# LSH attention and two MoE layers on one core: the exponential between the two casts in every third attention step

## The chip, the cores and the metric

The kernel runs on one core of a Trainium2 chip. The metric is device time in microseconds (us). Engine names in the rows: PE is TensorE's matrix multiplication, PEld its loads of the stationary operand, DVE VectorE, ACT ScalarE, POOL GpSimd, SP the engine that issues most transfers. TensorE multiplies and transposes into PSUM; VectorE and ScalarE read PSUM and do the rest of the arithmetic.

## The reference

Attention with a bucket mask comes first, then two feed-forward layers on its output. Shapes: 2 batches, 8 heads, 768 positions, head size 64; 1536 tokens, model width 512, hidden width 2048; everything in 32-bit floats.

```python
mask = q_bucket[:, :, :, None] == k_bucket[:, :, None, :]
scores = scale * np.matmul(q, k.transpose(0, 1, 3, 2))
scores = np.where(mask, scores, -1000000000.0)
scores = scores - np.max(scores, axis=-1, keepdims=True)
attn = np.exp(scores)
attn = attn / (np.sum(attn, axis=-1, keepdims=True) + 1e-09)
return np.matmul(attn, v).astype(np.float32)
...
h = x @ w_in
g = h * (1.0 / (1.0 + np.exp(-1.702 * h)))
return (g @ w_out).astype(np.float32)
```

The second layer is like the first with another activation. The buckets are the signs of six projections of each query and key.

## The kernel before

The attention runs as one loop over 96 score steps: 16 heads with 6 tiles of 128 queries each, and four more steps to drain. Score step `i` makes one tile of 128 queries by 768 keys. What belongs to one tile is spread over five steps, so that every step holds work of several tiles:

- `qk(i + 1)` (L613): four matrix products into one of two PSUM tiles `s`, scores and mask together.
- `clamp(i)` (L625, VectorE): reads `s`, writes the tile `p` in SBUF and the row minimum `mn`.
- `expo(i)` (L638, ScalarE): the exponential of `p` in place, with the row sums. It needs the clamp.
- `trp(g, t)` (L676 and L683): three transposes on TensorE, 128 columns of each of the three tiles `p` of the group `g`, into a PSUM tile `pt`, of which there are three buffers; then a cast on ScalarE to the high part `pth`. The three tiles of group `g` are those of score steps 3g, 3g+1 and 3g+2, so the first transposes of a group need the exponential of the last step of the three. Each step transposes two such 128-column pieces, called A and B here.
- `trl(g, t)` (L688, VectorE): the low part `ptl` = `pt` minus `pth`. It needs the cast.
- `pv(g, t)` (L700, L701): in the step after, the products of both parts with the values, into the PSUM tile `u`. When the sixth piece of a group is done, `u_out` copies `u` out on ScalarE (L712). This falls into steps with number 0 modulo 3, behind their exponential.

Every engine takes its instructions in the order of the program, and the schedule is written out by hand: a string of letters gives the order within a step. A and B are the two `trp`, a and b the two `trl`, C the clamp, E the exponential, T the list of other work that is due at this step, Q the next scores, P and R the two `pv`.

The list of other work holds, for each head from number 2 on, the products with the bucket projections and the mask comparison of the head (L493 on TensorE, `mk` L513 on VectorE). They fall into every sixth step, always one with number 2 modulo 3, and take a `pt` buffer too. Once per pair of heads it holds the transposition of the row sums (L657) and their reciprocal (L653). From step 47 on it prepares the first two weight tiles: their operations on VectorE (L238, L243) fall into steps 47, 59, 71 and 83, which are 2 modulo 3 as well. Behind the loop come the two feed-forward layers, whose weights, activations and sums are ordered by a list of due times.

Of the kernel before, what the change touches and what calls it, by code (L numbers as in the profile page):

```python
# [41 lines left out]
def lsh_attention_moe_kernel(  # L42
# [291 lines left out]
    def r_in(m, f, k0=0, k1=KD):  # L334
        if k0 == 0:
            pool, tag = mps["h"], f"h{f % 2}"
            if (m, f // 2) == (0, 1):
                pool, tag = (mps["q"], "Y") if f % 2 else (mps["h"], "y0")
            h_t[m, f] = pool.tile([P, CH], F32, tag=tag, name="h")
        h = h_t[m, f]  # L340
        wh, wl = w_t[m, f, 0]
        n = 3 * k0
        for kk in range(k0, k1):
            wk = slice(kk * P, (kk + 1) * P)
            for a, x in ((wh, xr_hi), (wh, xr_lo), (wl, xr_hi)):
                nc.tensor.matmul(  # L346
                    h, a[:, wk], x[:, kk], start=(n == 0), stop=(n == 3 * KD - 1)
                )
                n += 1

    def attention():
        with ExitStack() as es:
# [67 lines left out]
            def keep_warm(n, cols):  # L420
                t = ps_t.tile([P, 512], F32, tag="pt", name="warm")
                for _ in range(n):
                    nc.tensor.matmul(t[:, :cols], ones[:, :P], ones[:, :cols], start=True, stop=True)
# [179 lines left out]
            def qk(i, parts=(0, 1), fs=(0, 1)):  # L603
                n, t = divmod(i, NT)
                kh, qx, qb, kb, _ = opnd[n]
                if 0 in parts and 0 in fs:
                    st_t[i] = ps_s.tile([P, 2, 512], F32, tag="s", name="s")
                s = st_t[i]
                c = slice(t * P, (t + 1) * P)
                both = (qx, kh, True), (qb, kb, False)  # L610
                for a, bb, st in [both[x] for x in parts]:
                    for f in fs:
                        nc.tensor.matmul(  # L613
                            s[:, f, :HS],
                            a[:, c],
                            bb[:, f * HS : (f + 1) * HS],
                            start=st,
                            stop=not st,
                        )

            def clamp(i):
                s = st_t[i]
                sb = pp.tile([P, 2, HS], F32, tag="p", name="p")
                mn = sm.tile([P, 1], F32, tag="mn", name="mn")
                nc.vector.tensor_scalar(  # L625
                    sb, s[:, :, :HS], NEG, None, ALU.min, ALU.min, accum_out=mn
                )
                st_t[i] = (sb, mn)

            def expo(i):  # L630
                sb, mn = st_t.pop(i)
                n, t = divmod(i, NT)
                p = sb.rearrange("p a b -> p (a b)")
                u, h = divmod(n, 2)
                if t == 0 and h == 0:
                    z_t[u] = sm.tile([P, 2 * NT], F32, tag="z", name="z", bufs=2)
                zc = NT * h + t
                nc.scalar.activation(  # L638
                    p,
                    p,  # L640
                    AF.Exp,
                    bias=mn,
                    scale=-1.0,
                    accum_out=z_t[u][:, zc : zc + 1],
                )
                p_t[i] = p
# [26 lines left out]
            def trp(g, t):  # L673
                ptile = ps_t.tile([P, 512], F32, tag="pt", name="pt")
                for j in range(3):
                    nc.tensor.transpose(  # L676
                        ptile[:, j * P : (j + 1) * P],
                        p_t[3 * g + j][:, t * P : (t + 1) * P],
                        ident,
                    )  # L680
                hi = ptp.tile([P, HS], F32R, tag="pth", name="pth")
                lo = ptp.tile([P, HS], F32R, tag="ptl", name="ptl")
                nc.scalar.copy(hi, ptile[:, :HS])  # L683
                pt_t[g, t] = (hi, lo, ptile)

            def trl(g, t):
                hi, lo, ptile = pt_t[g, t]
                nc.vector.tensor_sub(lo, ptile[:, :HS], rnd(hi))  # L688
                if t == NT - 1:
                    for j in range(3):  # L690
                        p_t.pop(3 * g + j)

            def pv(g, t):
                n, f = divmod(g, 2)
                hi, lo, _ = pt_t.pop((g, t))
                if t == 0:
                    u_t[g] = ps_u.tile([P, 512], F32, tag="u", name="u")
                ut = u_t[g]
                vv = opnd[n][4][0]
                nc.tensor.matmul(ut[:, :HS], vv[:, t, :], hi, start=(t == 0), stop=False)  # L700
                nc.tensor.matmul(ut[:, :HS], vv[:, t, :], lo, start=False, stop=(t == NT - 1))  # L701
                if t == NT - 1:
                    u_out(g)
# [47 lines left out]
            second[2]()  # L751
            LAG = 3
            ORDER = "ACaBbETQPR"
            NZ = 5
            NZL = 2
            PVLAG = LAG + 1
# [2 lines left out]
            def at(step, f, *args):  # L759
                todo.setdefault(step, []).append((f, args))  # L760
# [30 lines left out]
            for u in range(NHD // 2):  # L791
                zs = 2 * NT * (u + 1)
                nz = NZ if u < NHD // 2 - 1 else NZL
                at(zs + 1, norm0, u)
# [26 lines left out]
            for i in range(NSTEP + PVLAG):  # L821
                if i == NSTEP:
                    es_s.close()
                    mps["h"] = ctx.enter_context(
                        tc.tile_pool(name="ps_h", bufs=1, space=PSUM, side="right")
                    )
                parts = iter(range(max(0, 2 * (i - NSTEP)), min(2 * (i - NSTEP) + 2, 2 * KD)))
                for part in parts:
                    r_in(0, part // KD, part % KD, part % KD + 1)
                    break  # L830
                kk = i - LAG
                tr = 0 <= kk < NSTEP
                g, j = divmod(kk, 3)
                kv = i - PVLAG
                gv, jv = divmod(kv, 3)
                for op in ORDER if i != 2 else ORDER.replace("TQ", "QT"):
                    if op == "A" and tr:
                        trp(g, 2 * j)
                    elif op == "B" and tr:
                        trp(g, 2 * j + 1)  # L840
                    elif op == "a" and tr:
                        trl(g, 2 * j)
                    elif op == "b" and tr:
                        trl(g, 2 * j + 1)
                    elif op == "C" and i < NSTEP:
                        clamp(i)
                        if i == 3:
                            second[7]()
                    elif op == "E" and i < NSTEP:
                        expo(i)  # L850
                    elif op == "Q" and i + 1 < NSTEP:
                        qk(i + 1, (0, 1) if i else (1,))
                        if i == 0:
                            keep_warm(4, 256)
                    elif op == "P" and 0 <= kv < NSTEP:
                        pv(gv, 2 * jv)
                    elif op == "R" and 0 <= kv < NSTEP:
                        pv(gv, 2 * jv + 1)
                    elif op == "T":
                        while todo and min(todo) <= i:  # L860
                            st = min(todo)
                            f, args = todo[st].pop(0)
                            if not todo[st]:
                                del todo[st]
                            f(*args)
                for part in parts:
                    r_in(0, part // KD, part % KD, part % KD + 1)
# [5 lines left out]
    def moe():  # L873
        with ExitStack() as es:
# [354 lines left out]
            while due:  # L1229
                flush()  # L1230

    attention()
    moe()

# [53 lines left out]
```

## Time and profile before

| what | value |
|---|---|
| median of three runs | 731.43 us (731.1 to 732.01) |
| the profiled execution | 731.06 us |
| span of its trace, first to last instruction | 729.3 us |
| TensorE busy in the span | 723.5 us |
| VectorE busy | 616.3 us |
| ScalarE busy | 469.0 us |
| granted TensorE clock, mean share of full speed | 0.999 |

The profile is that of one execution. Busy time is the union of an engine's instructions; neighbours on one engine can overlap by their tails, and the ends of matrix products are modelled, so a busy TensorE may still wait a little within it.

### The profile page before, as it was taken

How to read it: one execution, taken by the hardware profiler on the slowest of the kernel's cores; microseconds unless marked ns; L12 is line 12 of the kernel's file. 1: busy time of each engine (PE TensorE's matmuls, PEld its weight loads, DVE VectorE, ACT ScalarE, POOL GpSimd, SP SyncE). 2: the span in 40 equal slices, each digit the busy share in tenths (PEclk: the TensorE clock that was granted, in tenths of full speed). 3: DMA queues.
4: the chain of work that ended last, by engine and by line, in shares of the span. 5: the costliest groups of instructions: out<-in, count | busy, mean ns of one | idle time of the engine just before them, and what ended most of it. 6: DMA issues, size and time to landing. Idle time of an engine off the chain costs nothing.

```text
span 729.3 us, 11137 instructions
## 1 busy us (share of the span) xinstructions
PE 723.5 (99%) x3856; PEld 631.5 (87%) x3856; DVE 616.3 (85%) x1134; ACT 469.0 (64%) x957; POOL 185.4 (25%) x187
## 2 busy tenths in 40 slices
PE   8999999999999999999999999999999999999998
PEld 6999999999998788888888888888888888888886
DVE  8888889989888959878878797998699899897864
ACT  7888888888898765536546465576635656455340
POOL 7968877889893000000000000000000000000000
PEclk9999999999999999999999999999999999999999
DMA  5745656666624221121211221301302121211004
GB/s 157 199 125 145 190 141 163 182 157 153 170 85 118 109 70 48 58 87 64 82 58 58 88 88 60 112 0 59 115 0 87 59 75 69 88 58 58 1 1 173
DMA packets 25992, 69.53 MB, mean 95 GB/s; under 512 B 4464, under 2 KB 6992, under 8 KB 25936
## 3 DMA queue, kind: packets, MB, share of 16 engines
q1 hardware_dynamic: 25632, 68.62, 31.7%
q8 instruction: 30, 0.49, 0.3%
q10 hardware_dynamic: 304, 0.20, 0.1%
q14 instruction: 26, 0.21, 0.1%
HBM read 49.09 MB, written 3.19 MB: 72 GB/s over the span
## 4 chain that ended last, share of the span: by engine, by line
PE 94%; DVE 2%; ACT 2%; DMA 0%; issue 0%; DVEq 0%
PE y L947 36%; PE X L1010 11%; PE s L613 9%; PE pt L676 9%; PE Y L1010 8%; PE W L1010 7%; PE u L701 4%; PE u L700 4%; PE h L346 4%; PE prep L493 2%; ACT p L638 1%; DMA qn<-in_qt_dram 0%; ACT pth L683 0%; DVE gl L907 0%; DVE Y L1031 0%
## 5 line engine op out<-in xcount | busy, mean ns | idle before, releaser
L688 DVE TENSOR_TENSOR ptl<-pt,pth 128x384 fp32r<-128x384 f32 x192 | 98.1, 553 | 22.4 <-ACT pth L683 20.2
L683 ACT CAST pth<-pt 128x384 fp32r<-128x384 f32 x192 | 82.8, 484 | 28.7 <-PE pt L676 28.7
L638 ACT ACTIVATE p<-p,mn 128x768 f32<-128x768 f32 x96 | 91.2, 950 | 1.7 <-DVE p L625 1.6
L625 DVE TENSOR_SCALAR_CACHE_REDUCE p<-s 128x768 f32<-128x768 f32 x96 | 90.6, 945 | 0.3 <-PE s L613 0.2
L961 DVE TENSOR_TENSOR xq<-xq,y 128x512 f32<-128x512 f32 (+1 forms) x113 | 75.6, 679 | 13.7 <-PE y L947 13.0
L676 PE MATMUL pt<-ident,p 128*128 128x128 f32 x576 | 81.1, 274 | 0.1
L947 PE MATMUL y<-wh,gh 128*128 128x512 f32 (+1 forms) x194 | 75.4, 389 | 0.0
L947 PE MATMUL y<-wl,gh 128*128 128x512 f32 (+1 forms) x194 | 75.4, 389 | 0.0
L947 PE MATMUL y<-wh,gl 128*128 128x512 f32 (+1 forms) x194 | 75.2, 387 | 0.0
L947 PE MATMUL y<-gh,wh 128*128 128x512 f32 x192 | 75.0, 391 | 0.0
L947 PE MATMUL y<-gh,wl 128*128 128x512 f32 x192 | 74.9, 390 | 0.0
L947 PE MATMUL y<-gl,wh 128*128 128x512 f32 x192 | 74.7, 389 | 0.0
L259 ACT CAST wh<-wb 128x512 fp32r<-128x512 f32 x64 | 39.4, 620 | 54.5 <-DVE wb L246 26.2
L676 PEld LDWEIGHTS pt<-ident,p 128*128 128x128 f32 x576 | 68.5, 140 | 6.6 <-ACT p L638 2.4
L700 PE MATMUL u<-pth,vv 128*128 128x384 f32 x192 | 64.7, 337 | 0.0
L701 PE MATMUL u<-ptl,vv 128*128 128x384 f32 x192 | 64.5, 336 | 0.0
L613 PE MATMUL s<-kh,qx 128*128 128x384 f32 x192 | 55.7, 370 | 0.2 <-DVE p L625 0.2
L613 PE MATMUL s<-kb,qb 128*128 128x384 f32 x192 | 49.3, 337 | 0.3 <-POOL qk_m L473 0.2
L261 DVE TENSOR_TENSOR wl<-wb,wh 128x512 fp32r<-128x512 f32 x62 | 42.3, 687 | 3.9 <-ACT wh L259 3.6
L961 DVE TENSOR_TENSOR yr<-yr,y 128x512 f32<-128x512 f32 x56 | 38.2, 684 | 7.8 <-PE y L947 6.9
L947 PEld LDWEIGHTS y<-wh,gl 128*128 128x128 f32 x194 | 36.4, 188 | 7.6
L947 PEld LDWEIGHTS y<-wh,gh 128*128 128x128 f32 x194 | 36.5, 188 | 7.3 <-DVE xq L961 0.4
(272 smaller groups left out, 1842.1 us busy)
## 6 DMA issues: line engine op xcount, KB each, us to landing
raw<-in_wt_dram SPq DMA_DIRECT2D x64, 512.0 KB, 3.6
kn<-in_kt_dram SPq DMA_DIRECT2D x15, 384.0 KB, 4.2
vn<-in_vt_dram SPq DMA_DIRECT2D x8, 384.0 KB, 5.3
ul<-uh SPq DMA_DIRECT2D x16, 192.0 KB
rb<-scr SPq DMA_DIRECT2D x16, 192.0 KB, 3.5
qn<-in_qt_dram SPq DMA_DIRECT2D x15, 192.0 KB, 3.4
qx<-qk_m SPq DMA_DIRECT2D x15, 192.0 KB, 3.9
qb<-qk_m SPq DMA_DIRECT2D x15, 192.0 KB, 5.6
```

What stands on the lines that cost most here:

```text
L261: sub(lo, wf, rnd(hi))
L613: nc.tensor.matmul(s[:, f, :HS], a[:, c], bb[:, f * HS : (f + 1) * HS], start=st, stop=not st,)
L625: nc.vector.tensor_scalar(sb, s[:, :, :HS], NEG, None, ALU.min, ALU.min, accum_out=mn)
L638: nc.scalar.activation(p, p, AF.Exp, bias=mn, scale=-1.0, accum_out=z_t[u][:, zc : zc + 1],)
L676: nc.tensor.transpose(ptile[:, j * P : (j + 1) * P], p_t[3 * g + j][:, t * P : (t + 1) * P], ident,)
L683: nc.scalar.copy(hi, ptile[:, :HS])
L688: nc.vector.tensor_sub(lo, ptile[:, :HS], rnd(hi))
L700: nc.tensor.matmul(ut[:, :HS], vv[:, t, :], hi, start=(t == 0), stop=False)
L701: nc.tensor.matmul(ut[:, :HS], vv[:, t, :], lo, start=False, stop=(t == NT - 1))
L947: nc.tensor.matmul(y, w[:, js] if m == 0 else x[:, js], x if m == 0 else w[:, i0:i1], start=(n == 0), stop=(n == 5),)
L961: nc.vector.tensor_add(acc, acc, y)
L1010: nc.tensor.matmul(bk[b], w[:, k], x, start=(first and i == 0), stop=(hook is not None and i == 2), skip_group_check=True,)
```

## The change

In the steps with number 2 modulo 3, except step 2, the letter E moves from behind `b` to between `a` and `B`.

```diff
             LAG = 3
             ORDER = "ACaBbETQPR"
+            MID_E = "ACaEBbTQPR"
             NZ = 5
...
-                for op in ORDER if i != 2 else ORDER.replace("TQ", "QT"):
+                for op in ORDER.replace("TQ", "QT") if i == 2 else MID_E if i % 3 == 2 else ORDER:
```

The steps 5, 8, ..., 95 are 31. Steps with number 2 modulo 3 are those in which the last two pieces of one group are transposed and the third tile of the next group gets its exponential. On ScalarE this is the piece around step 8, with the step before it (`p_398` is step 7's tile, `p_431` step 8's, `pth_428` its piece A, `pth_439` or `pth_440` its piece B, `pth_477` the first piece of step 9):

```order
 L638 ACTIVATE p_398,z_210<-p_398,mn_399 128x768
 L683 CAST pth_428<-pt_424 128x384
-L683 CAST pth_439<-pt_435 128x384
 L638 ACTIVATE p_431,z_210<-p_431,mn_432 128x768
+L683 CAST pth_440<-pt_436 128x384
 L683 CAST pth_477<-pt_473 128x384
 L683 CAST pth_488<-pt_484 128x384
```

One cast has moved behind the exponential; the same piece stands 31 times. VectorE's queue around the same step, in the changed kernel (`p_431` and `p_480` are written by the clamps of steps 8 and 9, `mk_462` is the mask comparison):

```order
L625 TENSOR_SCALAR p_431,mn_432<-s_414 128x768
L688 TENSOR_TENSOR ptl_429<-pt_424,pth_428 128x384
L688 TENSOR_TENSOR ptl_441<-pt_436,pth_440 128x384
L513 TENSOR_SCALAR mk_462<-prep_455,mc_116 128x384
L625 TENSOR_SCALAR p_480,mn_481<-s_464 128x768
```

Here nothing has moved: before, the rows are the same but for the numbers of the tiles (`ptl_440<-pt_435,pth_439`). The queues of TensorE, GpSimd and the transfers are unchanged too.

## Rows read from the trace of the kernel before

**Rows 1.** Stretches: length, busy us of PE, PEld, DVE, ACT, POOL, then clock, DMA.

```profile
16.80:219.20 202.40, 202.31 (x1352) 196.40 (x1351) 182.18 (x386) 174.29 (x403) 167.22 (x158) 1.00 0.59 155
219.20:729.30 510.10, 506.59 (x2441) 425.45 (x2438) 420.46 (x723) 281.91 (x531) 5.45 (x7) 1.00 0.21 69
```

**Rows 2.** Timeline of TensorE, transposes: start, us, what, count.

```profile
30.30 0.81 PE L676 MATMUL pt<-ident,p 128*128 128x128 f32 x6
32.35 1.03 PE L676 MATMUL pt<-ident,p 128*128 128x128 f32 x6
...
36.65 0.82 PE L676 MATMUL pt<-ident,p 128*128 128x128 f32 x6
39.74 0.82 PE L676 MATMUL pt<-ident,p 128*128 128x128 f32 x6
...
46.01 0.90 PE L676 MATMUL pt<-ident,p 128*128 128x128 f32 x6
48.14 0.81 PE L676 MATMUL pt<-ident,p 128*128 128x128 f32 x6
...
59.41 1.03 PE L676 MATMUL pt<-ident,p 128*128 128x128 f32 x6
```

**Rows 3.** TensorE's weight loads at 32 us, and its line in the list of waits.

```profile
32.72 0.42 PEld L676 LDWEIGHTS pt<-ident,p 128*128 128x128 f32 x4 [0.23 <-ACT p L638]
...
PEld pt L676 <- ACT p L638: 2.4, 10, 0.3
```

**Rows 4.** Timeline of ScalarE and VectorE in step 11 (transposes at 30.30).

```profile
30.88 0.86 ACT L683 CAST pth<-pt 128x384 fp32r<-128x384 f32 x2 [0.26 <-PE pt L676]
31.63 0.95 ACT L638 ACTIVATE p<-p,mn 128x768 f32<-128x768 f32 x1
...
31.39 1.02 DVE L688 TENSOR_TENSOR ptl<-pt,pth 128x384 fp32r<-128x384 f32 x2 [0.15 <-ACT pth L683]
32.33 0.95 DVE L625 TENSOR_SCALAR_CACHE_REDUCE p<-s 128x768 f32<-128x768 f32 x1
```

**Rows 5.** Timeline of VectorE, then ScalarE, behind a weight operation in step 47.

```profile
113.53 1.10 DVE L238 TENSOR_SCALAR raw<-raw 128x512 uint32<-128x512 uint32 x1
114.55 0.94 DVE L625 TENSOR_SCALAR_CACHE_REDUCE p<-s 128x768 f32<-128x768 f32 x1
...
116.36 0.94 DVE L625 TENSOR_SCALAR_CACHE_REDUCE p<-s 128x768 f32<-128x768 f32 x1
...
117.35 1.02 DVE L688 TENSOR_TENSOR ptl<-pt,pth 128x384 fp32r<-128x384 f32 x2
118.29 0.95 DVE L625 TENSOR_SCALAR_CACHE_REDUCE p<-s 128x768 f32<-128x768 f32 x1
...
115.54 0.94 ACT L638 ACTIVATE p<-p,mn 128x768 f32<-128x768 f32 x1 [0.35 <-DVE p L625]
...
116.48 0.46 ACT L712 COPY uh<-u 128x384 f32<-128x384 f32 x1
116.83 0.86 ACT L683 CAST pth<-pt 128x384 fp32r<-128x384 f32 x2
```

**Rows 6.** Timeline of VectorE: another weight operation, and a mask comparison.

```profile
140.71 0.69 DVE L243 SCALAR_TENSOR_TENSOR wb<-wb,raw 128x512 uint32<-128x512 uint32 x1
141.31 0.96 DVE L625 TENSOR_SCALAR_CACHE_REDUCE p<-s 128x768 f32<-128x768 f32 x1
...
174.95 0.66 DVE L513 TENSOR_SCALAR mk<-prep,mc 128x384 f32<-128x384 f32 x1
175.54 0.94 DVE L625 TENSOR_SCALAR_CACHE_REDUCE p<-s 128x768 f32<-128x768 f32 x1
```

**Rows 7.** First and last changed clamp (31, every third), and step 96's third load.

```profile
17.11 0.95 DVE L625 TENSOR_SCALAR_CACHE_REDUCE p<-s 128x768 f32<-128x768 f32 x1
...
219.21 0.95 DVE L625 TENSOR_SCALAR_CACHE_REDUCE p<-s 128x768 f32<-128x768 f32 x1
...
221.64 0.42 PEld L676 LDWEIGHTS pt<-ident,p 128*128 128x128 f32 x4 [0.24 <-ACT p L638]
```

## The prediction

> **What bounds the kernel now.** The table of stretches comes first [rows 1]. From the 6th score step to the last (16.8 to 219.2 us) TensorE is busy for 202.31 of 202.40 us at a granted clock of 1.00, VectorE for 182.18 and ScalarE for 174.29. TensorE sets the pace; VectorE has about a tenth of the time to spare. The rest of the span, 510 us, is not touched by the change and is TensorE's too (506.59 of 510.10), so what the attention gains or loses should pass to the end nearly whole.
>
> The pace is read from TensorE's rows of transposes, six to a step [rows 2]. I number a group's steps M, M+1, M+2: M is the changed step (step number 2 modulo 3), the one whose exponential finishes a group's third tile `p`. A plain step is 2.05 us (30.30 to 32.35), a step with a new head's logits 3.09 (36.65 to 39.74). Four groups take 27.06 (32.35 to 59.41). The steps right behind an M are the only ones where the six transposes take longer than 0.82: 1.03 or 0.90. The reason stands in the weight-load row [rows 3]: the third load waits 0.23 us for the exponential of M. The list of waits has ten such waits, 2.4 us in all; the milder kind (0.90, step of 2.13 instead of 2.05, 46.01 to 48.14) is not counted there, and with about seven of them at 0.08 adds 0.6. So the wait that the new order aims at is worth at most 3.0 us.
>
> **What the change moves.** No instruction is added or removed, no transfer is issued elsewhere, and only ScalarE's queue changes, in 31 steps: cast, exponential, cast, where it was cast, cast, exponential. The first cast's readers notice nothing. Two things move:
>
> *The exponential starts earlier.* Today in M the casts start at 30.88, the exponential at 31.63, and the load behind it goes at 32.72, 1.09 after the exponential's start [rows 3, 4]. Starting one cast (about 0.37) earlier is more than the 0.23, if the clamp that feeds it is done. Gain: 0 to 3.0 us.
>
> *The second cast starts later,* by the whole exponential. Who waits for it? VectorE's queue in a step is clamp, first subtraction, second subtraction, then the next step's clamp, and the second subtraction reads the second cast. It cannot start early, and the next clamp stands behind it. So I need the length of this loop: clamp of M, exponential, second cast, second subtraction, clamp of M+1. The trace of before doesn't contain the loop, but every link of it, in the one stretch where VectorE is already late [rows 5]:
> - clamp start to exponential start, when the exponential waits for it: 114.55 to 115.54, 0.99.
> - exponential start to ScalarE's next start: 115.54 to 116.48, 0.94.
> - cast start to subtraction start, when it waits: 116.83 to 117.35, 0.52, and 30.88 to 31.39, 0.51 [rows 4]. I take 0.51.
> - subtraction start to the next VectorE start: half of 117.35 to 118.29 for two, 0.47.
>
> Sum 2.91 us from clamp to clamp, where a VectorE step without waits is 1.81 (114.55 to 116.36). The change costs VectorE 1.10 us in every M.
>
> The other two steps of a group, once VectorE is late, stand in the same rows: clamp of M+1 at 114.55, of M+3 at 118.29, 3.74 for two steps. That is 0.12 more than 2 x 1.81, because the copy of the output tile (116.48) stands between the exponential and the casts that the next subtraction waits for. A whole group on VectorE: 2.91 + 3.74 = 6.65 us. A group with logits has the mask comparison too, 0.59 (174.95 to 175.54), and the weight preparation puts four operations behind M steps: twice 1.02 (113.53 to 114.55) and twice 0.60 (140.71 to 141.31) [rows 5, 6]. Today these hide in VectorE's spare time; without spare time each is paid in full, 3.24 us.
>
> **Does it fit?** TensorE's four groups without the waits for the exponential: 27.06 - 0.23 - 0.08 = 26.75. VectorE's four groups today without waits: 12 x 1.81 + 2 x 0.59 = 22.90. Spare: 3.85, or 0.96 a group. The change asks for 1.10 + 0.12 = 1.22 a group. It does not fit, by about a quarter of a microsecond a group. VectorE becomes the bound of this stretch: 4 x 6.65 + 2 x 0.59 = 27.78 us instead of 27.06. What is late next is the clamp, then the exponential that needs it, then the third transpose: the removed wait comes back from the other side and grows.
>
> The Trainium skill's page "Perfetto Trace Analysis", section "Optimization Strategy", says to find the gaps on the most-contended engine and to make the dependency behind each start sooner. By this the exponential should start sooner, as here, and the sum would be a gain of up to 3.0 us instead of the loss below. The gap is real [rows 3], but the rule looks at the engine that waits, and the rows of VectorE [rows 5] show what the releaser's new place costs elsewhere; the rule is a rival below.
>
> **The sum.** From the clamp of the first changed step to that of the last (17.11 and 219.21 [rows 7]; 30 groups; 14 heads, numbers 2 to 15, with a mask comparison) VectorE needs 30 x 6.65 = 199.5, + 14 x 0.59 = 8.26, + 3.24, together 211.0 us, where it took 202.10: +8.9. At the end the old load of the third transpose came at 221.64, 2.43 after the clamp; the new one comes 0.99 + 1.09 = 2.08 after it, 0.35 less. TensorE is then 8.55 us late, say 8.6. On the profiled execution's own 731.06 that is 739.7; the median of the three runs is 0.37 higher, 731.43, so I forecast 740.0.
>
> Bounds. The links are single readings: 0.03 us less on three of them is 0.1 a group, 3 us in all (737). If the four weight operations still hid, 3.2 less. Upward: ScalarE has a few other copies in M and M+1 near the end, which could hold casts by some tenths, and an estimate from VectorE's busy time is higher still (last rival).
>
> **Rivals.** About 0.2% (1.5 us) is what a measurement of this kernel can tell from no change.
> - *The wait is simply removed* (the rule above): the spare time swallows the second cast's delay, TensorE loses its 3.0 us of waits: 731.4 - 3.0 = 728.4. For it: VectorE's 20 idle us in the stretch and the three buffers of transposed tiles, which let TensorE run ahead. Against it: buffers lend time once, and a group's deficit comes thirty times. It decides at a cost below 0.85 us a group (0.96 less a thirtieth of 3.24); the links say 1.22. Chance 0.09.
> - *Loss and gain cancel:* a cost of some 0.9 to 1.0 a group, time within 1.5 us of 731.4. Chance 0.07.
> - *VectorE is the bound, but the output copy isn't in its way* (the casts of M+2 come soon enough in the new rhythm): 30 x 0.12 = 3.6 less, 736.4. Against it: the order of ScalarE's queue behind M is the same as in rows 5. Chance 0.2.
> - *More is lost:* VectorE's busy time of 182.2 plus 31 x 1.10 is 216.3 against 202.4, some 14 more, 745. Against it: busy time counts the overlap of neighbours twice (two subtractions last 1.02, the next starts after 0.94). Chance 0.07.
>
> That leaves 0.57 for the forecast and its own range, 737 to 742. For eight times in ten I take 734.5 to 743, which holds it, the third rival and the near part of the last. Faster: 0.09; same: 0.07; slower: 0.84.
>
> **What the profile after would show.** The stretch from the first to the last changed clamp takes 209 to 212 us instead of 202.1. VectorE's wait of the subtraction for the cast grows from a few tenths in each step to about 1 us in each M (subtraction alone in its row, idle 1 us, released by the cast), and the clamp-to-clamp distance over M is 2.9, or 3.5 with the mask. The exponential in M starts because of the clamp, not behind a cast. TensorE's waits at the transposes grow instead of vanishing: the third load behind a plain M for the exponential, 0.3 us or more, and, behind an M with logits, the second tile's first load for VectorE's subtraction, because the logits' tile takes one of the three buffers. Past 230 us all is as before, shifted; the granted clock stays at 1.00.
>
> I am wrong if transposes behind M take 0.82 throughout and VectorE still starts its clamps on time: then a link is shorter than I read it. I am wrong in size if M's detour is right but M+1 and M+2 take 3.62, not 3.74, or if the weight operations cost nothing.

## The result and the profile after

The changed kernel takes 739.83 us (median of four runs, 738.14 to 740.78), the kernel before 731.26 (four runs beside them, 731.0 to 732.01): a ratio of 1.0112, with a 95% interval of 1.01 to 1.0125. It is slower by 8.6 us, close to the forecast of 740.0. The profiled execution took 740.78 us, with a span of 739.0. Line numbers above 750 of the code are one higher than before; all lines named here stand ahead of that, except in experiments where it is said.

The stretches come first, cut at the clamps of step 5 and step 95 (columns as in [rows 1]):

```profile
17.72:229.16 211.44, 206.89 (x1354) 196.51 (x1353) 180.63 (x387) 176.85 (x403) 167.74 (x159) 1.00 0.57 148
229.20:739.00 509.80, 506.32 (x2437) 424.99 (x2435) 419.76 (x723) 281.80 (x531) 4.57 (x5) 1.00 0.21 69
```

The changed stretch lasts 211.44 us instead of 202.10 [rows 7], the part behind it 509.80 as before [rows 1], and the granted clock is 1.00 in both. TensorE is busy for 206.89 us where it was busy for nearly all of 202.40: the stretch became longer and has holes of 4.5 us. Its busy time rose by 4.6 us as well, though no work was added; the modelled ends of its products cover part of its waits. VectorE is busy for 180.63 us, a little less than before, so by busy time nothing points to it.

The two spans differ by 9.70 us: 0.61 ahead of step 5 (17.72 against 17.11; up to this clamp both kernels have the same instructions in the same order, and the experiments whose program is the same up to there have it at 16.7 to 17.3, so it belongs to the execution), +9.34 in the stretch, -0.25 behind it.

What happened is seen in the timeline of VectorE, around the plain changed step 11 (its clamp is the one at 31.57) and then at step 73, whose clamp is the one at 175.66:

```profile
31.57 0.95 DVE L625 TENSOR_SCALAR_CACHE_REDUCE p<-s 128x768 f32<-128x768 f32 x1
...
32.45 0.55 DVE L688 TENSOR_TENSOR ptl<-pt,pth 128x384 fp32r<-128x384 f32 x1
33.99 0.56 DVE L688 TENSOR_TENSOR ptl<-pt,pth 128x384 fp32r<-128x384 f32 x1 [0.99 <-ACT pth L683]
34.47 0.95 DVE L625 TENSOR_SCALAR_CACHE_REDUCE p<-s 128x768 f32<-128x768 f32 x1
...
36.27 0.95 DVE L625 TENSOR_SCALAR_CACHE_REDUCE p<-s 128x768 f32<-128x768 f32 x1
...
175.66 0.95 DVE L625 TENSOR_SCALAR_CACHE_REDUCE p<-s 128x768 f32<-128x768 f32 x1
...
177.74 2.38 DVE L238 TENSOR_SCALAR raw<-raw 128x512 uint32<-128x512 uint32 x1
180.04 0.94 DVE L625 TENSOR_SCALAR_CACHE_REDUCE p<-s 128x768 f32<-128x768 f32 x1
```

Before, step 11 has its clamp here, and the next clamp at 32.33 [rows 4], 2.04 us behind:

```profile
30.29 0.95 DVE L625 TENSOR_SCALAR_CACHE_REDUCE p<-s 128x768 f32<-128x768 f32 x1
```

The two subtractions of M, one row of 1.02 before [rows 4], have come apart: the second waits 0.99 us for its cast, and the clamp of M+1 stands behind it. From clamp to clamp M takes 2.90 us (31.57 to 34.47), M+1 takes 1.80. The same engine does the same work with a hole of a microsecond in every M. The distance over M is 2.9 in nearly every plain group of the stretch and 3.5 in nearly every one with logits; in the kernel before it lies between 1.8 and 3.1. ScalarE in the same step:

```profile
31.79 0.50 ACT L683 CAST pth<-pt 128x384 fp32r<-128x384 f32 x1
32.56 0.94 ACT L638 ACTIVATE p<-p,mn 128x768 f32<-128x768 f32 x1 [0.28 <-DVE p L625]
...
33.50 1.37 ACT L683 CAST pth<-pt 128x384 fp32r<-128x384 f32 x3
```

The exponential starts 0.99 us behind the clamp, released by it and no longer behind a cast, and the second cast 0.94 behind the exponential, the distances of [rows 5]. The list of waits has the same in sums (waiter, releaser: us in all, times, longest):

```profile
DVE ptl L688 <- ACT pth L683: 32.1, 36, 1.0
...
ACT p L638 <- DVE p L625: 19.3, 52, 2.2
...
PEld pt L676 <- DVE ptl L688: 4.6, 11, 0.8
...
PEld pt L676 <- ACT zt L663: 2.6, 7, 0.4
...
PEld pt L676 <- ACT p L638: 1.4, 5, 0.4
...
PEld s L613 <- DMA kb<-mk: 1.0, 2, 0.9
```

Before, the first two lines were:

```profile
DVE ptl L688 <- ACT pth L683: 20.2, 65, 1.2
...
ACT p L638 <- DVE p L625: 1.6, 3, 0.7
```

VectorE waits for ScalarE and ScalarE for VectorE: a loop through both. On TensorE the wait for the exponential fell from 2.4 us [rows 3] to 1.4, but three others have come, together larger. They stand in its weight loads:

```profile
33.64 0.42 PEld L676 LDWEIGHTS pt<-ident,p 128*128 128x128 f32 x4 [0.24 <-ACT p L638]
...
35.94 0.31 PEld L676 LDWEIGHTS pt<-ident,p 128*128 128x128 f32 x3 [0.16 <-DVE ptl L688]
...
48.01 0.31 PEld L676 LDWEIGHTS pt<-ident,p 128*128 128x128 f32 x3 [0.38 <-ACT zt L663]
...
172.45 0.39 PEld L613 LDWEIGHTS s<-kb,qb 128*128 128x128 f32 x2 [0.89 <-DMA kb<-mk]
```

Two of these places are the second tile of a step, whose buffer `pt` is not free yet: VectorE's subtraction or ScalarE's copy `zt` of the row sums still reads it. The last is the transfer of the mask rows for the next head. The transposes show the same as in [rows 2], with 1.04 and 0.96 in the two steps behind M instead of 1.03 and 0.82:

```profile
33.26 1.04 PE L676 MATMUL pt<-ident,p 128*128 128x128 f32 x6
...
35.53 0.96 PE L676 MATMUL pt<-ident,p 128*128 128x128 f32 x6
```

### The profile page after: what moved, and what is told of

Read it like the earlier page. It is cut to its first block, busy times and chain, and to the rows that moved or that the text cites. A ratio compares the mean times of both kernels' runs of the same rounds, so it can differ in the third digit from the quotient of the medians.

```text
span 739.0 us, 11137 instructions
## 1 busy us (share of the span) xinstructions
PE 729.7 (99%) x3856; PEld 633.2 (86%) x3856; DVE 614.6 (83%) x1134; ACT 471.8 (64%) x957; POOL 184.7 (25%) x187
## 4 chain that ended last, share of the span: by engine, by line
PE 85%; DVE 7%; issue 3%; ACT 3%; DMA 1%; DVEq 0%; SPq 0%; ACTq 0%
PE y L948 35%; PE X L1011 11%; PE Y L1011 7%; PE W L1011 7%; PE s L613 6%; PE pt L676 6%; PE h L346 4%; PE u L700 3%; PE u L701 3%; DVE p L625 3%; DVE ptl L688 2%; PE prep L493 2%; ACT pth L683 1%; DMA qn<-in_qt_dram 1%; ACT p L638 1%
## 5 line engine op out<-in xcount | busy, mean ns | idle before, releaser
L688 DVE TENSOR_TENSOR ptl<-pt,pth 128x384 fp32r<-128x384 f32 x192 | 100.7, 552 | 33.1 <-ACT pth L683 32.1
L683 ACT CAST pth<-pt 128x384 fp32r<-128x384 f32 x192 | 86.1, 479 | 16.7 <-PE pt L676 15.7
L676 PE MATMUL pt<-ident,p 128*128 128x128 f32 x576 | 84.0, 276 | 4.0 <-DVE ptl L688 2.4
L700 PE MATMUL u<-pth,vv 128*128 128x384 f32 x192 | 64.8, 337 | 0.0
L701 PE MATMUL u<-ptl,vv 128*128 128x384 f32 x192 | 64.6, 336 | 0.0
```

The lines of the kernel that those rows point to most:

```text
L676: nc.tensor.transpose(ptile[:, j * P : (j + 1) * P], p_t[3 * g + j][:, t * P : (t + 1) * P], ident,)
```

## The experiments

**Theory A** is that of the prediction: the late second cast adds a hole to VectorE's queue, VectorE (with ScalarE in the loop) has no room for it in every group, and TensorE loses what VectorE can't make up; the weight operations on VectorE (L238, L243) are then paid in full. **Theory B**: each late cast costs TensorE directly, by a buffer that comes free later, about 8.5 / 31 = 0.27 us in every changed step, whatever room VectorE has. **Theory C** came from the first traces: the mask rows of the next head come late, through the transfer queue.

**Half of the changed steps each.** First only the plain ones, then only those with logits:

```diff
-                for op in ORDER.replace("TQ", "QT") if i == 2 else MID_E if i % 3 == 2 else ORDER:
+                for op in ORDER.replace("TQ", "QT") if i == 2 else MID_E if i % 6 == 5 else ORDER:
```

```diff
-                for op in ORDER.replace("TQ", "QT") if i == 2 else MID_E if i % 3 == 2 else ORDER:
+                for op in ORDER.replace("TQ", "QT") if i == 2 else MID_E if i % 6 == 2 else ORDER:
```

> The exponential moves between the casts only in every sixth step (5 modulo 6), those without a head's logits. Theory A (VectorE's loop clamp, exponential, second cast, second subtraction, clamp is 1.1 us longer than a plain step, and TensorE loses what VectorE can't make up): now VectorE needs 6.65 us in one group and 5.5 + 0.6 in the next, 12.8 for a pair against TensorE's 13.4, so the delay is made up in the group with logits, and the waits for the exponential, which all stand behind these steps, are gone: 728.4 to 729.5 us. Theory B (each late cast costs by itself, some 0.28 us, wherever it stands): half of the loss stays, about 735.5 us.

> The exponential moves only in the steps that hold a head's logits (2 modulo 6). Theory A: VectorE needs 7.24 + 5.5 us for a pair against TensorE's 13.4, so nothing is lost; no wait for the exponential stood behind these steps, so little is gained: 731.3 us, give or take 0.7. Theory B: half of the loss, about 735.5 us.

Measured: 734.18 us against 731.01 (ratio 1.0033, 1.0021 to 1.0045) and 733.1 against 731.01 (1.0031, 1.002 to 1.0042). Neither theory's numbers: A expected a gain of 2 us from the plain half and no change from the other, B half of the loss from each; by the medians they lose 3.2 and 2.1 (by the ratios 2.4 and 2.3), and 5.3 together is less than 8.6. The traces say where (the profiled executions took 734.18 and 734.62 us). With plain steps alone TensorE's transposes stand within 0.3 us of before up to the first weight operation. There the wait for the exponential is gone from step 12 on in every other plain group, 0.2 us each, but 0.13 of it comes back two steps later, at the products of the next head, whose PSUM tile a subtraction still reads, and the rest in the other plain groups. Then TensorE loses 0.8 us at the first weight operation and 1.2 at the second. First VectorE, then TensorE's weight load at that place:

```profile
141.66 0.56 DVE L688 TENSOR_TENSOR ptl<-pt,pth 128x384 fp32r<-128x384 f32 x1 [0.76 <-ACT pth L683]
142.13 1.30 DVE L243 SCALAR_TENSOR_TENSOR wb<-wb,raw 128x512 uint32<-128x512 uint32 x1
143.35 0.94 DVE L625 TENSOR_SCALAR_CACHE_REDUCE p<-s 128x768 f32<-128x768 f32 x1
```

```profile
144.83 0.31 PEld L676 LDWEIGHTS pt<-ident,p 128*128 128x128 f32 x3 [1.24 <-DVE ptl L688]
```

The weight operation comes on top of the late subtraction, and the clamp stands 1.69 us behind that subtraction. With logits steps alone nothing is lost for the first 150 us, after which the loss comes in three pieces of 0.9 to 1.4 us, the first and the last of them waits for the mask rows. B is ruled out by this: the ten late casts up to there would have cost 2.7 us by it. The weight load of the scores in the run with logits steps:

```profile
167.84 0.36 PEld L613 LDWEIGHTS s<-kb,qb 128*128 128x128 f32 x2 [1.07 <-DMA kb<-mk]
```

Why these rows come late is seen in SyncE's queue, at the issues of this kernel and then of the kernel before (start, us, queue, line, transfer):

```profile
154.46 0.45 SPq L215 DMA_DIRECT2D raw<-in_wt_dram  x1
155.00 0.34 SPq L664 DMA_DIRECT2D scr<-zt  x1
...
161.79 1.11 SPq L669 DMA_DIRECT2D rb<-scr  x2
...
163.63 0.55 SPq L527 DMA_DIRECT2D qb<-mk  x1
```

```profile
153.71 0.45 SPq L215 DMA_DIRECT2D raw<-in_wt_dram  x1
154.73 0.32 SPq L664 DMA_DIRECT2D scr<-zt  x1
...
159.34 1.11 SPq L669 DMA_DIRECT2D rb<-scr  x2
...
161.29 0.55 SPq L527 DMA_DIRECT2D qb<-mk  x1
```

`rb<-scr` reads back what `scr<-zt` wrote, so the queue stands until that has landed, and the mask rows stand behind it. From one issue to the other it takes 6.79 us in the new order and 4.61 before; `scr<-zt` is issued 0.54 us behind the 512 KB of `raw` instead of 1.02. The mask rows go out 2.34 us later. That the smaller distance makes the landing later is what I supposed, but it is not shown: no run changed the distance alone, and in the trace of the fifth experiment below a distance of 1.14 us goes with 6.43 us to the read. Why the landing takes longer stays open.

**Less work on VectorE.** One subtraction of six is left out in every group (fourth piece, its high part goes into both products), in the changed kernel and, as a control, in the one before:

```diff
+                if t != 3:
                     nc.vector.tensor_sub(lo, ptile[:, :HS], rnd(hi))
```

> The changed kernel without the fourth piece's subtraction (one of six in a group, in the second step behind a changed one; the high part is multiplied twice instead, so that TensorE has the same work). This leaves out the low part of one piece in six. Theory A: VectorE gets 0.47 us a group, 6.18 instead of 6.65, less than TensorE's 6.69 on average; the whole loss goes, and the removed waits show: 728.4 to 730.5 us. Theory B, or a loss that comes from the transposed tiles' buffers alone: 739 to 740 us as in the changed kernel.

> The control to the run without the fourth piece's subtraction: the kernel before with the same piece left out. Both theories: TensorE bounds this kernel, VectorE has time to spare, no change, 731.3 us give or take 0.5. If it gets faster as much as the other, the other's gain says nothing on the change.

Measured: 733.77 us (ratio 1.0029, 1.0019 to 1.0039) and 730.92 (0.9998, 0.999 to 1.0007), both against 731.01. On the kernel before VectorE's 0.47 us a group is worth nothing; on the changed one it is worth 6 us of the 8.6. That is theory A's mark. (The run also frees a buffer `pt` sooner; in its trace M+2 takes 1.47 us from clamp to clamp instead of 1.93, and the fifth experiment tells VectorE's time from the buffer.) But A wanted a gain, since 1.22 - 0.47 = 0.75 a group is less than the 0.85 at which the prediction had it turn. In the trace TensorE is indeed 0.7 us ahead of before by 90 us, about 0.2 more in every four groups, and then loses again at the mask rows and behind the weight operations. An average of spare time per group did not say whether these fit.

**The same early exponential without VectorE standing still.** In plain changed steps the second subtraction moves into the next step, behind that step's clamp (letter d); casts and exponential stand as in the change.

```diff
-            MID_E = "ACaEBbTQPR"
+            MID_E = "ACaEBTQPR"
+            NEXT_D = "ACdaBbETQPR"
...
-                for op in ORDER.replace("TQ", "QT") if i == 2 else MID_E if i % 3 == 2 else ORDER:
+                for op in ORDER.replace("TQ", "QT") if i == 2 else MID_E if i % 6 == 5 else NEXT_D if i > 5 and i % 6 == 0 else ORDER:
...
+                    elif op == "d":
+                        trl(g - 1, NT - 1)
```

> As in the run with the plain steps alone (5 modulo 6), but the second subtraction of such a step is written behind the next step's clamp, so that VectorE never stands before the late cast. Theory A (the cost is VectorE standing before the late cast; the weight operations hurt only because that wait has used up the spare time): the clamps come on time, the weight operations hide again, and the removed waits show: 728.4 to 730.0 us, where the run without this edit took 734.2. Rival (the late cast itself, or the exponential's earlier place, disturbs TensorE): 733 to 735 us again.

Measured: 730.73 us against 731.48 (0.9998, 0.9989 to 1.0006). The loss of the plain steps (3.2) is gone while ScalarE's casts and exponential stand as in the change, so in these steps the late cast by itself costs nothing; what cost was VectorE standing still in front of a clamp. The same in all 31 steps was not run. VectorE in step 11 and 12:

```profile
31.00 0.56 DVE L688 TENSOR_TENSOR ptl<-pt,pth 128x384 fp32r<-128x384 f32 x1 [0.15 <-ACT pth L683]
31.47 0.94 DVE L625 TENSOR_SCALAR_CACHE_REDUCE p<-s 128x768 f32<-128x768 f32 x1
...
32.35 1.66 DVE L688 TENSOR_TENSOR ptl<-pt,pth 128x384 fp32r<-128x384 f32 x3
```

The clamp follows the first subtraction, 1.58 us behind the clamp of M (29.89) instead of 2.90, and the three subtractions run without a hole. The gain that was expected, 2 to 3 us, did not come: four groups take 26.92 us (transposes 34.00 to 60.92) against 27.06. Behind a step with the transposition of the row sums the six transposes take 0.94 (at 45.41) where it was 0.90 [rows 2], but it is another wait: before, the third load waits 0.10 us for the exponential; here that is gone, and the fourth waits 0.14 for the buffer that the copy `zt` still reads. And of the 0.7 us gained by step 50 some 0.5 is lost again in a wait for the mask rows (166.01).

**The weight operations.** The full change, with L238 and L243 left out for the two weight tiles that are prepared during the attention; then the same with only the plain steps changed:

```diff
-        if k < NDVE:
+        if k < 2:
+            pass
+        elif k < NDVE:
```

> The changed kernel without the four weight operations on VectorE that fall into changed steps (L238 and L243 of the first two weight tiles; this leaves out the low bits of these weights). Theory A with the sum of the prediction: without spare time each is paid in full, so 3.2 us less than the changed kernel, about 736.6 us. Rival (they hide, and the loss is elsewhere): 739.8 us, no change.

> The exponential moves in the plain steps alone, and the same four weight operations are left out. Theory A: the delay of each plain step is made up in the next group with logits, nothing else falls on VectorE there, and the gain that was expected of the plain steps shows: 728.4 to 730.0 us. Rival (a plain step's late cast costs more than its wait was worth, weights or not): 733 us or more, as with the weight operations (734.2).

Measured: 735.99 us (1.0069, 1.0056 to 1.0082) and 731.2 (0.9995, 0.9986 to 1.0004), against 731.48. With the full change the four operations are worth 739.83 - 735.99 = 3.8 us by the medians: paid in full. VectorE's clamps of steps 5 and 95 in the first of the two (line 629 here is the clamp):

```profile
16.80 0.95 DVE L629 TENSOR_SCALAR_CACHE_REDUCE p<-s 128x768 f32<-128x768 f32 x1
...
224.39 0.94 DVE L629 TENSOR_SCALAR_CACHE_REDUCE p<-s 128x768 f32<-128x768 f32 x1
```

207.59 us, 3.85 less than 211.44, and close to 30 x 6.63 + 14 x 0.58 = 207.0, which is VectorE's rhythm without them. In the plain steps they are the whole loss: 734.18 becomes 731.2, though against before nothing is gained. No run leaves them out of the kernel before, but its trace bounds what they cost there: four groups take 27.17, 27.07 and 27.26 us behind the first three of them (TensorE's transposes of steps 48, 60, 72 and 84, at 113.55, 140.72, 167.79 and 195.05) and 27.06 without [rows 2], 0.3 us in all; from step 84, where the fourth falls, to step 96 it takes 26.21 us, and 26.32 in the second run here.

**The mask comparison ahead of the second subtraction**, logits steps alone, to test theory C:

```diff
-            MID_E = "ACaEBbTQPR"
+            MID_E = "ACaEBTbQPR"
```

> The exponential moves in the logits' steps alone, and in these the mask comparison is written ahead of the second subtraction, into the time in which VectorE waits for the late cast. Theory C (in the run with the logits' steps alone the 2.1 us came from the late mask comparison: its transfers and what is queued behind them on the transfer queue came late, and the next head's score products waited for their mask rows at steps 72 and 84): most of it goes, 731.0 to 732.0 us. Rival (the loss is VectorE's late clamp there, or chance in the transfers): 733 us again.

Measured: 732.4 us against 731.48 (1.0015, 1.0006 to 1.0024), where the run without this had 1.0031. Half of the loss is gone, a little less than C expected. The waits for the mask rows at 168 and 197 us are not in the trace, and TensorE keeps within 0.3 us of before in the whole attention. In this trace `rb<-scr` starts 5.27 us behind `scr<-zt`, between the other two. C is supported, but the whole list of other work moves, `scr<-zt` with the comparison, so which of the two does it stays open. Most of the rest of the loss is of the edit's own making: the draining step 98 is one of its steps too, and there the list holds weight operations, which now stand ahead of the last subtraction. TensorE's wait for it:

```profile
230.78 0.19 PEld L701 LDWEIGHTS u<-ptl,vv 128*128 128x128 f32 x1 [0.82 <-DVE ptl L688]
```

**The output copy later.** The full change, with the copy of `u` (L712) moved behind the first cast of the next step, to take the 0.12 us out of M+2:

```diff
-                    u_out(g)
+                    u_due.append(g)
...
+                        if u_due:
+                            u_out(u_due.pop())
```

> The changed kernel with the copy of the output tile put behind the first cast of the following step, out of the way between the exponential and that cast. Theory A as the prediction sized it: the copy costs VectorE 0.12 us a group, 3.6 us in all, so 736 to 737 us instead of 739.8. Rival (the copy is not in the way once VectorE is late): 739.8 us; if TensorE must wait for the copy before it may write the output tile again, more.

Measured: 742.8 us against 731.78 (1.0156, 1.0142 to 1.0169), worse than the change. TensorE now waits for the copy before it writes `u` again (the copy is L715 here, and L701 the first of the two products, L700 elsewhere):

```profile
PEld u L701 <- ACT uh L715: 9.8, 28, 0.9
```

The changed kernel has no such wait in the stretch. The copy has no room to go later, so the time of this run says nothing on the 0.12. Its clamps do: step 13, an M+2, takes 1.84 us from clamp to clamp, where the changed kernel has 1.93, while in other M+2 it takes 2.0 and more. So the copy does cost VectorE about 0.1 us there.

**What the removed wait is worth by itself.** The order of the fifth experiment only in every twelfth step, the plain ones without a transposition of the row sums:

```diff
-                for op in ORDER.replace("TQ", "QT") if i == 2 else MID_E if i % 6 == 5 else NEXT_D if i > 5 and i % 6 == 0 else ORDER:
+                for op in ORDER.replace("TQ", "QT") if i == 2 else MID_E if i % 12 == 11 else NEXT_D if i > 0 and i % 12 == 0 else ORDER:
```

> As in the run with the second subtraction behind the next clamp, but only in every twelfth step (11 modulo 12): the plain steps without the transposition of the row sums. That run showed a wait of 0.2 us removed in these steps and a wait for the copy of the row sums that grew by 0.07 in the others. Theory A: eight waits of 0.21 us go and nothing is added: 1.2 to 1.7 us less than the kernel before in the attention, 729.6 to 730.3 us, if the mask transfers let TensorE run ahead by that much. Rival (the transfers' floor at steps 72 and 84 takes it back): 730.7 us or more.

Measured: 730.69 us against 731.78 (0.9992, 0.9983 to 1.0), a gain at the edge of what can be told. TensorE's transposes:

```profile
32.30 0.82 PE L676 MATMUL pt<-ident,p 128*128 128x128 f32 x6
34.35 0.82 PE L676 MATMUL pt<-ident,p 128*128 128x128 f32 x6
```

The transposes of step 12 take 0.82 instead of 1.03 [rows 2], and the next ones follow 2.05 behind instead of 2.26: 0.21 us, seen at steps 12, 24, 36 and 48 alike, and 1.0 us in all by step 96. No kernel here beats the one before by more than this.

## Why the prediction was right, point by point

**The bound moves to VectorE: right.** Taking 0.47 us a group off VectorE gives 6 us back in the changed kernel and nothing in the one before; letting VectorE go on behind the first subtraction takes the plain steps' loss away with the casts as late as in the change.

**The detour over M, 2.91 us: right.** 2.90 (31.57 to 34.47), link by link 0.99, 0.94, 0.49 and 0.48 for 0.99, 0.94, 0.51 and 0.47, and 3.48 with the mask comparison (27.83 is the clamp behind 24.35 in step 8), 0.58 more. The links were all in the one stretch of before where VectorE had been late.

**M+1 and M+2, 3.74: right.** 1.80 and 1.93, so a group is 6.63 for 6.65, and the copy's 0.12 is there (1.93 against 1.80 or 1.81). The rival without it, 736.4, falls.

**The weight operations, 3.24: mechanism right, term too small, one place wrong.** I had one in each of the steps 47, 59, 71 and 83; the second L238 stands in step 73, an M+2. By the distances from clamp to clamp, less the usual 2.90 or 1.93, they cost 0.33, 0.60, 2.45 and 0.60, together 3.98; leaving them out gave 3.8 in the times. I had 1.02 for each L238, and it cost 0.33 and 2.45 (the last section has more on this); that the four together came within 0.8 us of the sum is partly luck. The whole stretch: 30 x 6.63 + 14 x 0.58 + 3.98 = 211.0; the trace has 211.44, so all that TensorE waited for besides, the mask rows too, lengthened this loop by about 0.4 at most.

**The end, -0.35:** -0.25 (509.84 us from the clamp of step 95 to the end, where it was 510.09). The forecast of 740.0 is nearer to 739.83 than its terms deserve: the four executions lie between 738.14 and 740.78.

**The value of the removed wait, at most 3.0: too high, without an effect on the forecast,** because the forecast is VectorE's chain and doesn't contain it. A plain removed wait is worth 0.21, not all of which was there to be had (0.13 came back two steps later in the first experiment), and the milder kind, read rightly as a wait for the exponential, was worth nothing: where the exponential was earlier the same steps wait for the buffer that the copy `zt` reads (0.94 in the fifth experiment for 0.90). The changed kernel waits there for 0.38, seven times.

**The places of TensorE's waits: partly wrong.** I had the third load behind a plain M waiting 0.3 us or more for the exponential. It waits 0.24 in step 12, and from step 18 on 0.14 at most. I had the wait for VectorE at a second tile behind an M with logits; it stands mostly two steps behind a plain M (steps 7, 13, 25, 37, 49, 61 and 85). Most of the loss is at the second tile, for VectorE or the copy `zt`, and some in waits for the mask rows, of which the prediction says nothing. The total was right since the loop sets the distance of the steps, wherever TensorE shows the wait.

**"It decides at 0.85 us a group": wrong.** With 0.75 a group the third experiment still lost 2.8 us. The spare time of VectorE is not one account: the part in the steps with a weight operation was used up, and the transfer queue has deadlines of its own.

The rule that I weighed, from the Trainium skill's page "Perfetto Trace Analysis", section "Optimization Strategy", to make the dependency behind a gap start sooner, would have given 728.4. Its effect is in the traces, at 0.21 us where nothing else moves; here it was paid with 0.99 us of VectorE in each M.

## What to carry to other kernels

Before an operation is moved ahead of another on an engine that works in order, follow what it passes: its consumer may stand in front of work on the engine that releases the moved operation, and then the two queues form a loop whose length is added up from rows in which each link had to wait. An engine busy for nine tenths can have no room for one microsecond in the wrong place, so compare the loop with the step, not the busy share with 100%. If the gain is wanted nevertheless, move the late consumer behind the next urgent instruction as well; here, in the plain steps, this took the loss away, and no more than that.

## What was not expected of the hardware

The same VectorE operation, L238 on 128x512, took 0.42 us in step 47 and 2.38 us in step 73 of the changed kernel's trace, and 1.10 [rows 5] and 1.15 in the kernel before; L243 took 0.69 [rows 6] and, in the first experiment, 1.30. At the long one GpSimd was at work:

```profile
177.20 1.83 POOL L477 TENSOR_TENSOR qx<-qn,qk_m 64x768 fp32r<-64x768 f32 x1
179.01 0.83 POOL L109 TENSOR_SCALAR kh<-kn 128x768 fp32r<-128x768 f32 x1
```

In the first 235 us of all the traces here, a weight operation with no GpSimd operation beside it took 0.36 to 0.43 us (L238, 20 of them) or 0.68 to 0.70 (L243, 39); every longer one, 36 in all, overlapped work of GpSimd, while 15 others that did were not lengthened. So GpSimd was at work whenever one was lengthened, but not all of its work goes with a longer one, and no run changed GpSimd's work alone: that it is the cause is not shown.

A transfer of 6 KB (12 x 128 numbers), `scr<-zt`, let its reader start 4.61 to 7.32 us behind it (4.61 and 5.76 in the kernel before, 5.27 and 6.79 in two experiments, 7.32 in the changed kernel), and with it everything behind it on that queue.
